# Pooled attention with a soft mixture of experts: a running maximum folded through PSUM, queries pooled in place, shared small buffers, a 24th early weight piece, and a new order of the instructions

## The chip, the cores and the metric

The kernel runs on one core of one Trainium2 chip. The metric is the device time of one execution in microseconds (us). Before the change it is 986.83 us, the median of three runs (986.08 to 987.94). The engines are named as the profile names them: PE is the matrix engine (PEld its weight loads), DVE the vector engine, ACT the scalar engine, POOL the general engine (GpSimd), SP the engine whose queue issues all the DMAs here.

## What is computed

Attention over 64 heads (batch 8, 8 heads, 1152 positions, 64 dimensions), where each two neighbouring queries are first averaged, so that 576 queries per head remain. Its output, 4608 rows of 512, goes through a soft mixture of 8 experts with 4 slots each.

```
q_pool = q.reshape(B, H, S // 2, 2, D).mean(axis=3)
scores = scale * q_pool @ k^T
attn   = softmax(scores, axis=-1)
x      = attn @ v                    # rows: all queries of all batches
logits = x @ phi                     # 32 slots
d      = softmax(logits, axis=0);  slot_input = d.T @ x
slot_out[e] = max(slot_input[e] @ w1[e], 0) @ w2[e]
c      = softmax(logits, axis=1);  out = c @ slot_out
```

All values are 32-bit floats.

## The kernel before

**Tiles.** Two heads form a pair (32 pairs, four of them in a batch). A pair's 576 pooled queries are cut into three units of 192, so there are 96 units, twelve in each of the eight batches. The keys lie in nine chunks of 128. A unit's scores are made in five tiles, of two chunks each and the last of one chunk, with keys on the partitions: a tile `sc` has the form 128 x (2 heads x up to 384) and takes two PSUM banks. There are two such tiles, used in turn.

**A unit, step by step**, with the names of the planner (left) and the tiles that a profile shows:

- `S`: PE makes a score tile (`sc<-qs,k`). A matmul of 32-bit data is recorded as two instructions, so a chunk of two heads is four.
- `C`: ACT copies the tile into SBUF (`s<-sc`).
- `X`: DVE takes the maximum of the tile and the running maximum `M` (`M<-sc,s` for the second tile, where the first is read from its copy in `s`, then `M<-sc,M`). `M` holds two maxima side by side, one for the even and one for the odd chunks. For the last tile, a single chunk, only the even half is touched.
- `Xf`, the fold: DVE takes the maximum of the two halves of `M` (`M<-M`). Before the change it stands between the fourth tile's `X` and the last one's.
- `mt`, `mc`, `mb`: the maximum over keys is finished by three PE transposes (`m<-ident,M`), a DVE reduction (`mc<-m`) and three transposes that spread it (`m<-ident,mc`).
- `sub`, `exp`: DVE subtracts (`s<-s,m`, three groups of three chunks), ACT takes the exponential (`s<-s`).
- `av`: PE multiplies with the values (`U<-s,v`, nine chunks); `add`: POOL adds up eight of the nine chunks (`cs`), and `sums`: PE sums the ninth and POOL's sum over the keys (`m<-s,ones`, `m<-cs,ones`).
- `tc`, `eps`, `rcp`, `tr`, `nx`: the denominator is turned (DVE `zt<-m`), offset (ACT `rc<-zt,eps`), inverted (DVE `rc<-rc`), spread (DVE `rr<-rc`) and multiplied in (POOL `xT<-rr,Us`), and ACT empties the `U` bank (`ue`: `Us<-U`).

**Loads.** For each pair SP issues loads of `k`, `q` and `v`. The raw queries `q` (both of a pair of neighbours, 576 KB) go into one buffer `qt`, and the sum of neighbours (`qs`) is written by POOL (by DVE for the first pair) into one of two buffers that belong to the even and the odd pairs. The two halves of the experts' weights come in 64 pieces of 512 KB. 23 of them have space during the attention and are loaded early; 21 more go into the space that the attention leaves; the last 20 take the place of pieces that have been used.

**The second stage.** When a batch's twelve units are done, the slots' logits, their exponentials and the weighted sums of the rows are made for that batch (`lT`, `eN`, `cN`, `xn`, `slot`), in between the next batch's units. After the last batch follow the experts (`b<-w,sT`, `b<-w,hT`) and the output (`ob`, 24 DMAs).

**What sets the order.** `graph` lists every step with its engine, an assumed cost, what it depends on and a due time made from the table `K["t"]`; `plan` walks through them, engine by engine, and takes among the steps that could start within a small tolerance (`K["wait"]`) the one with the earliest due time, where a matmul of the shape last used is favoured by `K["stay"]`. Each engine then runs its steps in the order that comes out. What an engine really waits for is set by semaphores.

Of the kernel before, what the change touches and what calls it, by code (L numbers as in the profile page):

```python
# [9 lines left out]
F32 = mybir.dt.float32  # L10
F32R = mybir.dt.float32r
AF = mybir.ActivationFunctionType
ALU = mybir.AluOpType
# [9 lines left out]
K = dict(  # L23
    unit=9.0,
    bufs=3,
    stay=97.457,
    wait=dict(PE=0.13, ACT=0.445, DVE=0.179, Pool=4.882),
    adds=(7, 7, 2),
    more=3,
    tiles=((0, 1), (2, 3), (4, 5), (6, 7), (8,)),  # L30
    groups=((0, 1, 2), (3, 4, 5), (6, 7, 8)),
    t=dict(
        S=(1044.713, -27.378, 661.778, 130.467, 574.088),
        C=(225.408, -176.587, 488.066, 26.318, 184.372),
        X=(-718.744, -301.904, -170.628, 686.571, 208.197),
        Xf=(730.727,),
        mt=(148.202,),
        mc=(-195.597,),
        mb=(131.38,),
        sub=(-1080.957, -16.471, 937.631),  # L40
        exp=(-1246.656, 343.957, 478.305),
        add=(-198.042, -184.679, 499.318, 714.631, 189.507, 204.651, 492.919, -541.643, -599.421),
        av=(778.115, -59.256, -118.326, -753.912, 731.892, 755.181, 926.264, 54.633, -257.777),
        sums=(248.993, -468.15, 546.677, -343.84, -281.108, -244.636, -433.554, -1124.137, 780.762, 473.892),
        ue=(756.065,),
        tc=(-949.47,),
        eps=(-191.284,),
        rcp=(26.863,),
        tr=(550.849,),
        ad2=(-53.911, -555.751, -604.838, -526.867, -758.418, 550.551, -1200.835, -328.898, -440.675),  # L50
        nx=(106.946,),
        ldk=(-619.286,),
        ldq=(598.38,),
        ldv=(-572.603,),
        qs=(673.048,),
        lg=(-347.354, 583.603, 769.132, 771.621),
        to=(568.435, 368.579, 194.047, -715.38),
        cb=(-19.617, 862.666),
        rm=(693.434, 659.42),
        nm=(-571.082,),  # L60
        ex=(723.911,),
        ns=(-235.664,),
        ce=(449.167,),
        cz=(641.165,),
        cm=(218.808,),
        on=(-345.56, 611.94, -1045.413, -114.604, -959.343, -369.874, 674.366, 739.505, 216.76, -1205.971, -784.9,
            231.495),
        we=(175.597, 148.186),
        ga=(550.866, 285.942, 446.335),
        end_lg=(297.494, 404.708, 205.171, -617.161),  # L70
        end_to=(-1060.395, 611.733, 617.206, 387.095),
        end_cb=(452.212, 686.767),
        end_rm=(-41.937, 690.132),
        end_nm=(-764.111,),
        end_ex=(794.722,),
        end_ns=(1693.028,),
        end_ce=(-656.049,),
        end_cz=(283.723,),
        end_cm=(-111.35,),
        end_on=(-245.398, -314.311, 700.307, -568.747, 642.619, -769.575, 431.084, 234.287),  # L80
        end_we=(196.041, -1145.853),
        end_ga=(619.182, -375.889, -765.507),
        fin_lg=(193.516, 208.183),
        fin_to=(-933.237, -176.561),
        fin_cb=(677.952, 123.947),
        fin_rm=(47.158,),
        fin_nm=(-321.662,),
        fin_ex=(537.275,),
        fin_ns=(474.34,),
        fin_ce=(684.257,),  # L90
        fin_cz=(538.018,),
        fin_cm=(778.587,),
        fin_on=(655.715, -822.063, -169.447, 107.564),
        fin_we=(557.048, -643.386),
        fin_ga=(827.62, -315.564, 319.142),
        fin_gs=(-237.215,),
    ),
)
LAT = 0.05
# [26 lines left out]
def graph(K, B, HP, NT3, Q, NW):  # L126
# [38 lines left out]
    for n in range(NP):  # L165
        lastu = NT3 * (n - 1) - 1
        k0 = None if n else first
        dma(("ldq", n), 2.0 if n else 0.6, [old(n, "qs", n - 1), ("qs2",) if n == 1 else None], k0)
        dma(("ldk", n), 2.0 if n else 0.8, [old(n > 1, "S", lastu, len(TI) - 1)], k0)
        if n == 0:  # L170
            dma(("k2",), 0.9, [], first)
            dma(("ldv", n), 2.0, [], first)
            dma(("q2",), 1.2, [], first)
            op(("qs2",), "DVE", dve_t((NT3 - 1) * Q), [("x", "q2")], key=0.0)
        else:
            dma(("ldv", n), 2.0, [old(n > 1, "av", lastu, NC - 1)])
        cost = pool_t(NT3 * Q) if n else dve_t(Q)
        op(("qs", n), "Pool" if n else "DVE", cost, [("x", "ldq", n), old(n > 1, "S", lastu, len(TI) - 1)])
    for u in range(NU):
        n, na = u // NT3, adds[u]  # L180
        for i, tl in enumerate(TI):
            g = len(TI) * u + i - 2
            d = [old(g >= 0, "C", g // len(TI), g % len(TI)), old(g >= 0 and g % len(TI), "X", g // len(TI), g % len(TI))]
            d += [("S", u, i - 1)] if i else [("qs", n), ("x", "ldk", n), old(u, "S", u - 1, len(TI) - 1)]
            d += [("x", "k2")] if u == 0 and tl[0] == KF else [("qs2",)] if (u, i) == (1, 0) else []
            op(("S", u, i), "PE", 0.00168 * Q * len(tl), d)
            d = [("S", u, i)]
            for c in tl:
                d += [("av", u - NB, c), freed(u - NB, c)] if u >= NB else []
            op(("C", u, i), "ACT", act_t(2 * Q * len(tl)), d)  # L190
            if i:
                before = ("X", u, i - 1) if 1 < i < len(TI) - 1 else ("C", u, 0) if i == 1 else ("Xf", u)
                op(("X", u, i), "DVE", dve_t(2 * Q * len(tl)), [("C", u, i), before] + [old(u and i == 1, "mt", u - 1)])
            if i == len(TI) - 2:
                op(("Xf", u), "DVE", dve_t(2 * Q), [("X", u, i)])
        b = ("m", u)
        op(("mt", u), "PE", 0.33, [("X", u, len(TI) - 1)], b, take=True)
        op(("mc", u), "DVE", (0.465, 0.55), [("mt", u), old(u > 1, "mb", u - 2)], b)
        op(("mb", u), "PE", 0.34, [("mc", u)], b)
        for g, cs in enumerate(GR):  # L200
# [126 lines left out]
    return order, start, max(free.values())  # L327


NW2 = 21  # L330
NW = 23


class InOrder:
# [15 lines left out]
def pooled_attention_soft_moe(ctx: ExitStack, tc: tile.TileContext, q, k, v, phi, w1, w2, out):  # L350
# [36 lines left out]

    SI4 = const.tile([P, 4, NS], F32, name="SI4")
    idv = ident.rearrange("p (g s) -> p s g", g=4)
    SI = const.tile([P, NS], F32, name="SI")  # L390
    nc.vector.tensor_reduce(SI, idv, axis=AX.X, op=ALU.add)
    for g in range(4):
        nc.vector.tensor_copy(SI4[:, g, :], SI)
    SI4f = SI4.rearrange("p g s -> p (g s)")
    phis = const.tile([P, HP, NS], F32, name="phis")
# [66 lines left out]
    class Pair:  # L462
# [11 lines left out]
            sp_q.dma_start(self.kt[:, KF * P:], k[self.n, :, KF * P:])  # L474

        def load_q(self):
            self.qt = ld.tile([P, 2, SP], F32, name=f"q{self.n}", tag="qt")
            n = SP if self.n else QU
            sp_q.dma_start(self.qt[:, :, :n], q[self.n, :, :, :n])

        def load_q2(self):
            sp_q.dma_start(self.qt[:, :, QU:], q[self.n, :, :, QU:])

        def load_v(self):
            self.vt = vp[self.n % 2].tile([P, 2, NC, D], F32, name=f"v{self.n}", tag="vt")
# [2 lines left out]
                sp_q.dma_start(phis, phi.rearrange("(c p) s -> p c s", p=P))  # L488

        def pool_q(self):  # L490
            self.qs = kp[self.n % 2].tile([P, SP], F32, name=f"qs{self.n}", tag="qs")
            n = SP if self.n else QU
            (pool if self.n else dve).tensor_tensor(self.qs[:, :n], self.qt[:, 0, :n], self.qt[:, 1, :n], op=ALU.add)

        def pool_q2(self):
            dve.tensor_tensor(self.qs[:, QU:], self.qt[:, 0, QU:], self.qt[:, 1, QU:], op=ALU.add)

    xTs = {}

    class Unit:  # L500
# [22 lines left out]
        def maxi(self, i):  # L523
            if i == 1:
                self.M = un.tile([P, 2, 2, QU], F32, name=f"M{self.u}", tag="M", bufs=1)
            n = len(TI[i])
            ps = self.ps[i][:, :, :n * QU].rearrange("p h (c q) -> p c h q", c=n)
            if n == 2:
                dve.tensor_tensor(self.M, ps, self.s[:, 0:2] if i == 1 else self.M, op=ALU.max)
            else:  # L530
                dve.tensor_tensor(self.M[:, 0], ps[:, 0], self.M[:, 0], op=ALU.max)

        def fold(self):
            dve.tensor_tensor(self.M[:, 0], self.M[:, 0], self.M[:, 1], op=ALU.max)

        def max_cols(self, bank):
            M = self.M[:, 0].rearrange("p h q -> p (h q)")
# [78 lines left out]
    class Moe:  # L616
# [11 lines left out]
        def logits(self, hf, phase, bank):  # L628
            cs, n = self.cols(hf)
            pl = mbank[bank]  # L630
            if phase == 0:
                if self.lT is None:
                    if self.last:
                        self.lT = sm.tile([P, self.nt * NQ], F32, name=f"lT{self.i}", tag="lTl", bufs=1)
                    else:
                        self.lT = sm.tile([P, SP], F32, name=f"lT{self.i}", tag="lT", bufs=1)[:, :self.nt * NQ]
                j0 = self.halves[hf][0]
                for hp in range(HP):
                    pe.matmul(pl[NS * hp:NS * hp + NS, :n], phis[:, hp, :], xTs[self.b][:, hp, j0 * NQ:j0 * NQ + n],
                              start=True, stop=True, skip_group_check=True, tile_position=(0, NS * hp))  # L640
            elif phase == 1:
                act.copy(self.lT[:, cs], pl[:, :n])
# [68 lines left out]
        def weights(self, phase, bank):  # L711
            if phase == 0:
                self.turned(bank)
            elif phase == 1:
                if self.last:
                    self.eN = sm.tile([NQ, self.nt, NS], F32, name=f"eN{self.i}", tag="eNl", bufs=1)
                else:
                    self.eN = sm.tile([NQ, NJ, NS], F32, name=f"eN{self.i}", tag="eN", bufs=1)[:, :self.nt]
                act.copy(self.eN, mbank[bank][:NQ, :self.nt * NS].rearrange("p (j s) -> p j s", j=self.nt))
# [244 lines left out]
```

## Time and profile before

One profiled execution took 987.6 us; its span from the first to the last instruction is 985.8 us. The kernel before has a median of 986.83 us.

| engine | busy us | share of the span | instructions |
|---|---|---|---|
| PE | 951.1 | 96% | 9358 |
| PEld | 676.1 | 69% | 9358 |
| DVE | 902.6 | 92% | 1307 |
| ACT | 762.3 | 77% | 1120 |
| POOL | 794.9 | 81% | 815 |

The page's second part shows the span in 40 slices of 24.6 us, each digit being the busy share in tenths:

```profile
PE   6999999999999999999999999999999999999995
...
DVE  5999999999999999999999999999999999999423
ACT  4878888888878888788878788778878788877323
POOL 2899888898889898898889988899888988888200
...
DMA  5132232232223222223122212121221221123898
```

Slices 2 to 37 are the attention with the second stage woven in: PE and DVE are nearly full throughout, DMA is light. In the last three slices, the experts and the output, DMA is full and DVE is not. A row of groups is read as line, engine, operation, out<-in, shapes, count | busy time, mean ns of one | idle time of the engine just before them and what ended it. All rows carry line 344, that of a helper that issues every instruction, so the names of the tiles tell the steps apart.

### The profile page before, as it was taken

How to read it: one execution, taken by the hardware profiler on the slowest of the kernel's cores; microseconds unless marked ns; L12 is line 12 of the kernel's file. 1: busy time of each engine (PE TensorE's matmuls, PEld its weight loads, DVE VectorE, ACT ScalarE, POOL GpSimd, SP SyncE). 2: the span in 40 equal slices, each digit the busy share in tenths (PEclk: the TensorE clock that was granted, in tenths of full speed). 3: DMA queues.
4: the chain of work that ended last, by engine and by line, in shares of the span. 5: the costliest groups of instructions: out<-in, count | busy, mean ns of one | idle time of the engine just before them, and what ended most of it. 6: DMA issues, size and time to landing. Idle time of an engine off the chain costs nothing.

```text
span 985.8 us, 23762 instructions
## 1 busy us (share of the span) xinstructions
PE 951.1 (96%) x9358; PEld 676.1 (69%) x9358; DVE 902.6 (92%) x1307; ACT 762.3 (77%) x1120; POOL 794.9 (81%) x815
## 2 busy tenths in 40 slices
PE   6999999999999999999999999999999999999995
PEld 4666777767776777677777677777776677776542
DVE  5999999999999999999999999999999999999423
ACT  4878888888878888788878788778878788877323
POOL 2899888898889898898889988899888988888200
PEclk8999999999999999999999999999999999999998
DMA  5132232232223222223122212121221221123898
GB/s 171 49 116 82 83 116 82 84 115 74 92 71 116 94 99 88 95 70 117 52 70 73 73 49 68 55 74 52 70 74 54 68 74 49 49 90 128 320 409 339
DMA packets 27681, 101.22 MB, mean 103 GB/s; under 512 B 3505, under 2 KB 4017, under 8 KB 27569
## 3 DMA queue, kind: packets, MB, share of 16 engines
q1 hardware_dynamic: 27568, 99.69, 29.4%
q8 instruction: 74, 1.21, 0.5%
q14 instruction: 39, 0.31, 0.1%
HBM read 90.24 MB, written 9.44 MB: 101 GB/s over the span
## 4 chain that ended last, share of the span: by engine, by line
PE 84%; DVE 12%; issue 1%; ACT 0%; DMA 0%; SPq 0%; DVEq 0%; ACTq 0%
PE sc L344 32%; PE U L344 27%; PE m L344 20%; DVE M L344 7%; PE b L344 5%; DVE s L344 2%; DVE zt L344 1%; DVE mc L344 1%; DVE slot L344 0%; DVE rc L344 0%; ACT s L344 0%; DMA k<-in_k_dram 0%; PE idle L344 0%; DVE c L344 0%; DVE rr L344 0%
## 5 line engine op out<-in xcount | busy, mean ns | idle before, releaser
L344 POOL TENSOR_TENSOR cs<-cs,s 128x384 f32<-128x384 f32 x571 | 586.8, 1028 | 61.7 <-ACT s L344 26.3
L344 ACT COPY s<-sc 128x768 f32<-128x768 f32 (+1 forms) x480 | 344.6, 733 | 91.8 <-PE sc L344 86.1
L344 PE MATMUL sc<-qs,k 64*128 64x192 f32 x3456 | 389.0, 349 | 20.9 <-DVE M L344 16.3
L344 DVE TENSOR_TENSOR s<-s,m 128x1152 f32<-128x1152 f32 x288 | 382.3, 1338 | 3.3 <-PE m L344 2.3
L344 ACT ACTIVATE s<-s 128x1152 f32<-128x1152 f32 x288 | 336.2, 1168 | 45.3 <-DVE s L344 45.1
L344 PEld LDWEIGHTS sc<-qs,k 64*128 64x128 f32 x3456 | 275.6, 188 | 117.0 <-issue 73.8
L344 PE MATMUL U<-s,v 128*64 128x192 f32 x3456 | 344.6, 333 | 0.9 <-ACT Us L344 0.9
L344 PEld LDWEIGHTS U<-s,v 128*64 128x64 f32 x3456 | 227.7, 136 | 73.3 <-issue 47.6
L344 DVE TENSOR_TENSOR M<-sc,M 128x768 f32<-128x768 f32 (+1 forms) x288 | 235.3, 817 | 6.3 <-ACT s L344 2.5
L344 POOL TENSOR_TENSOR cs<-s 128x384 f32<-128x384 f32 x96 | 96.8, 1008 | 33.9 <-ACT s L344 33.8
L344 DVE TENSOR_TENSOR M<-sc,s 128x768 f32<-128x768 f32 x96 | 91.0, 947 | 4.3 <-ACT s L344 4.3
L344 DVE TENSOR_TENSOR M<-M 128x384 f32<-128x384 f32 x96 | 71.2, 742 | 0.3
L344 POOL TENSOR_TENSOR xT<-rr,Us 128x192 f32<-128x192 f32 x95 | 57.1, 601 | 12.7 <-DVE rr L344 10.2
L344 POOL TENSOR_TENSOR qs<-q 128x576 f32<-128x576 f32 x31 | 54.6, 1761 | 13.3 <-DMA q<-in_q_dram 13.3
L344 DVE TENSOR_REDUCE mc<-m 128x3 f32<-128x384 f32 x96 | 53.4, 556 | 11.4 <-PE m L344 7.4
L344 PE MATMUL m<-ident,M 128*128 128x128 f32 x288 | 52.8, 293 | 0.0
L344 PE MATMUL m<-ident,mc 128*128 128x128 f32 x288 | 51.9, 289 | 0.0
L344 PE MATMUL m<-s,ones 128*64 128x192 f32 x388 | 48.7, 330 | 0.2 <-ACT s L344 0.2
L344 PE MATMUL m<-cs,ones 128*64 128x192 f32 x384 | 47.5, 326 | 0.0
L344 ACT COPY Us<-U 128x192 f32<-128x192 f32 x96 | 30.7, 320 | 21.7 <-PE U L344 20.9
L344 PEld LDWEIGHTS m<-ident,mc 128*128 128x128 f32 x288 | 29.2, 136 | 26.6 <-DVE mc L344 24.1
L344 PEld LDWEIGHTS m<-ident,M 128*128 128x128 f32 x288 | 30.1, 141 | 21.6 <-issue 21.6
(92 smaller groups left out, 499.6 us busy)
## 6 DMA issues: line engine op xcount, KB each, us to landing
w<-in_moe_w_dram SPq DMA_DIRECT2D x64, 512.0 KB, 5.4
v<-in_v_dram SPq DMA_DIRECT2D x32, 576.0 KB, 3.8
k<-in_k_dram SPq DMA_DIRECT2D x31, 576.0 KB, 3.8
q<-in_q_dram SPq DMA_DIRECT2D x31, 576.0 KB, 3.8
out_dram<-ob SPq DMA_DIRECT2D x24, 384.0 KB, 6.0
q<-in_q_dram SPq DMA_DIRECT2D x1, 384.0 KB, 6.4
k<-in_k_dram SPq DMA_DIRECT2D x1, 320.0 KB, 4.9
k<-in_k_dram SPq DMA_DIRECT2D x1, 256.0 KB, 2.9
```

Of the source, the lines that this page charges most:

```text
L344: return self.tc.keep_in_program_order(op(*args, **kwargs))
```

## The change

- **The fold.** `X` of the last tile writes its maximum back into the score tile in PSUM (`self.top`) instead of into `M`, and `Xf` now comes after it and takes the maximum of `self.top` and the odd half of `M`. So each of the two instructions has one operand in PSUM and one in SBUF, where before the fold had both in SBUF. The transposes `mt` depend on `Xf`, and so does the reuse of the score tile.
- **The queries.** Each load of `q` becomes two DMAs of half the size: one neighbour goes straight into the buffer `qs`, the other into a smaller `qt`, and the sum is made in place. The load therefore has to wait until the pair that used this `qs` buffer before has made its last scores, as the load of `k` already did.
- **Small buffers.** `SI` becomes the first quarter of `SI4` (three copies instead of four); for the last piece of the second stage `lT` and `eN` share the buffers of `zt` and `Us`.
- **The pieces.** With the space won, 24 pieces of weights are loaded early and 20 go into the space that the attention leaves.
- **The order.** All numbers of `K["t"]`, `stay` and `wait` are new.

```diff
 K = dict(
-    stay=97.457,
-    wait=dict(PE=0.13, ACT=0.445, DVE=0.179, Pool=4.882),
+    stay=344.932,
+    wait=dict(PE=0.084, ACT=0.259, DVE=0.255, Pool=0.318),
...
-        S=(1044.713, -27.378, 661.778, 130.467, 574.088),
+        S=(2388.548, -94.193, 2355.419, 2292.606, -219.496),
...
-        dma(("ldq", n), 2.0 if n else 0.6, [old(n, "qs", n - 1), ("qs2",) if n == 1 else None], k0)
+        dma(("ldq", n), 2.0 if n else 0.6, [old(n, "qs", n - 1), ("qs2",) if n == 1 else None, old(n > 1, "S", lastu, len(TI) - 1)], k0)
...
-        op(("qs", n), "Pool" if n else "DVE", cost, [("x", "ldq", n), old(n > 1, "S", lastu, len(TI) - 1)])
+        op(("qs", n), "Pool" if n else "DVE", cost, [("x", "ldq", n)])
...
+            d += [old(g >= 0 and g % len(TI) == len(TI) - 1, "Xf", g // len(TI))]
...
-                before = ("X", u, i - 1) if 1 < i < len(TI) - 1 else ("C", u, 0) if i == 1 else ("Xf", u)
+                before = ("X", u, i - 1) if i > 1 else ("C", u, 0)
...
-            if i == len(TI) - 2:
-                op(("Xf", u), "DVE", dve_t(2 * Q), [("X", u, i)])
+        op(("Xf", u), "DVE", dve_t(2 * Q), [("X", u, len(TI) - 1)])
...
-        op(("mt", u), "PE", 0.33, [("X", u, len(TI) - 1)], b, take=True)
+        op(("mt", u), "PE", 0.33, [("Xf", u)], b, take=True)
...
-NW2 = 21
-NW = 23
+NW2 = 20
+NW = 24
...
-    SI = const.tile([P, NS], F32, name="SI")
+    SI = SI4[:, 0, :]
...
-            self.qt = ld.tile([P, 2, SP], F32, name=f"q{self.n}", tag="qt")
-            n = SP if self.n else QU
-            sp_q.dma_start(self.qt[:, :, :n], q[self.n, :, :, :n])
+            self.qs = kp[self.n % 2].tile([P, SP], F32, name=f"qs{self.n}", tag="qs")
+            self.qt = ld.tile([P, SP], F32, name=f"q{self.n}", tag="qt")
+            self.q_part(slice(0, SP if self.n else QU))
+
+        def q_part(self, r):
+            sp_q.dma_start(self.qs[:, r], q[self.n, :, 0, r])
+            sp_q.dma_start(self.qt[:, r], q[self.n, :, 1, r])
...
-            (pool if self.n else dve).tensor_tensor(self.qs[:, :n], self.qt[:, 0, :n], self.qt[:, 1, :n], op=ALU.add)
+            (pool if self.n else dve).tensor_tensor(self.qs[:, :n], self.qs[:, :n], self.qt[:, :n], op=ALU.add)
...
-                dve.tensor_tensor(self.M[:, 0], ps[:, 0], self.M[:, 0], op=ALU.max)
+                self.top = ps[:, 0]
+                dve.tensor_tensor(self.top, self.top, self.M[:, 0], op=ALU.max)
 
         def fold(self):
-            dve.tensor_tensor(self.M[:, 0], self.M[:, 0], self.M[:, 1], op=ALU.max)
+            dve.tensor_tensor(self.M[:, 0], self.top, self.M[:, 1], op=ALU.max)
...
-                        self.lT = sm.tile([P, self.nt * NQ], F32, name=f"lT{self.i}", tag="lTl", bufs=1)
+                        self.lT = un.tile([P, self.nt * NQ], F32, name=f"lT{self.i}", tag="zt", bufs=1)
...
-                    self.eN = sm.tile([NQ, self.nt, NS], F32, name=f"eN{self.i}", tag="eNl", bufs=1)
+                    self.eN = un.tile([NQ, 3 * self.nt, NS], F32, name=f"eN{self.i}", tag="Us", bufs=1)[:, :self.nt]
```

What the table of numbers does is seen in the rows of each engine. The first place is DVE in a unit that has no work of the second stage beside it, in the middle of the run, before the change (the number behind a name tells one buffer or unit from another):

```order
L344 TENSOR_TENSOR M_4394<-sc_139,M_4394 128x768
L344 STREAM_TRANSPOSE zt_4439<-m_137 128x192
L344 TENSOR_TENSOR M_4394<-M_4394 128x384
L344 RECIPROCAL rc_4445<-rc_4445 128x6
L344 TENSOR_TENSOR M_4394<-sc_138,M_4394 128x384
L344 STREAM_TRANSPOSE rr_4460<-rc_4445 128x192
L344 TENSOR_TENSOR s_140<-s_140,m_135 128x1152
```

and DVE at the same place of the changed kernel:

```order
L344 TENSOR_TENSOR M_4399<-sc_137,M_4399 128x768
L344 STREAM_TRANSPOSE zt_4444<-m_133 128x192
L344 TENSOR_TENSOR sc_136<-sc_136,M_4399 128x2x192
L344 RECIPROCAL rc_4449<-rc_4449 128x6
L344 TENSOR_TENSOR M_4399<-sc_136,M_4399 128x384
L344 STREAM_TRANSPOSE rr_4464<-rc_4449 128x192
L344 TENSOR_TENSOR s_138<-s_138,m_135 128x1152
```

The neighbours are the same; the last tile's maximum now stands where the fold stood, and the fold where that maximum stood.

The second place is PE in such a unit, from its first matmuls with the values to the next unit's scores, before the change:

```order
L344 MATMUL U_5277<-s_142,v_4746 64x192 x8
L344 MATMUL sc_138<-qs_4934,k_4824 128x192 x4
L344 MATMUL U_5277<-s_142,v_4746 64x192 x2
L344 MATMUL sc_139<-qs_4934,k_4824 128x192 x2
L344 MATMUL U_5277<-s_142,v_4746 64x192 x2
L344 MATMUL m_137<-s_142,ones 64x192 x2
L344 MATMUL m_137<-cs_5215,ones 64x192 x2
L344 MATMUL U_5277<-s_142,v_4746 64x192 x6
L344 MATMUL sc_138<-qs_4934,k_4824 128x192 x4
L344 MATMUL sc_139<-qs_4934,k_4824 128x192 x4
L344 MATMUL m_136<-ident,M_5271 128x128 x3
```

and PE at this place of the changed kernel:

```order
L344 MATMUL U_5463<-s_139,v_5028 64x192 x8
L344 MATMUL sc_136<-qs_5108,k_5093 128x192 x4
L344 MATMUL U_5463<-s_139,v_5028 64x192 x2
L344 MATMUL sc_137<-qs_5108,k_5093 128x192 x2
L344 MATMUL m_135<-s_139,ones 64x192 x2
L344 MATMUL m_135<-cs_5398,ones 64x192 x2
L344 MATMUL U_5463<-s_139,v_5028 64x192 x8
L344 MATMUL sc_136<-qs_5108,k_5093 128x192 x4
L344 MATMUL sc_137<-qs_5108,k_5093 128x192 x4
L344 MATMUL m_135<-ident,M_5458 128x128 x3
```

One chunk of `U` has moved from ahead of the two sums to behind them, so the sums, and with them the read of POOL's `cs`, come one chunk earlier.

The third place is POOL where a pair's queries are summed, before the change:

```order
L344 TENSOR_TENSOR cs_6608<-s_142 128x384
L344 TENSOR_TENSOR cs_6608<-cs_6608,s_142 128x384
L344 TENSOR_TENSOR qs_6627<-q_6390 128x576
L344 TENSOR_TENSOR xT_5985<-rr_6641,Us_6639 128x192
L344 TENSOR_TENSOR cs_6608<-cs_6608,s_142 128x384 x5
```

and POOL there in the changed kernel:

```order
L344 TENSOR_TENSOR cs_6535<-cs_6535,s_139 128x384 x2
L344 TENSOR_TENSOR xT_5993<-rr_6573,Us_6571 128x192
L344 TENSOR_TENSOR cs_6535<-cs_6535,s_139 128x384 x4
L344 TENSOR_TENSOR qs_6549<-qs_6549,q_6550 128x576
L344 TENSOR_TENSOR cs_6633<-s_140 128x384
```

The sum of the queries has moved from among a unit's adds to the place between two units. At the start of the program SP now issues two loads of queries, not one, ahead of the first load of `k`.

More of the change, by code (lines that the diff above doesn't have):

```diff
@@ L32 @@
     t=dict(
-        S=(1044.713, -27.378, 661.778, 130.467, 574.088),
[L34 to L96, printed above, removed]
+        S=(2388.548, -94.193, 2355.419, 2292.606, -219.496),
+        C=(2649.137, 2739.454, 3306.242, 2568.215, 2210.822),
@@ new lines @@
+        X=(-718.744, 41.55, 2544.783, 3038.773, 3019.567),
+        Xf=(2420.829,),
+        mt=(108.212,),
+        mc=(2834.326,),
+        mb=(357.261,),
+        sub=(2554.368, 2777.459, 3141.454),
+        exp=(2989.515, 2742.131, 2760.717),
+        add=(-198.042, 2806.366, 2691.244, 2455.169, 2982.071, 2750.805, 2789.269, 2832.224, -599.421),
+        av=(2746.723, 2428.358, 2392.407, 122.273, 2706.594, 2907.997, 2728.152, 193.704, -87.967),
+        sums=(248.993, -468.15, 101.759, -343.84, -281.108, -244.636, -433.554, 32.153, 2812.114, 369.166),
@@ new lines @@
+        ue=(2111.732,),
+        tc=(2995.475,),
+        eps=(-193.75,),
+        rcp=(-83.517,),
+        tr=(2755.622,),
+        ad2=(-53.911, -555.751, -604.838, -526.867, 2247.684, 2996.492, 85.086, -328.898, -440.675),
+        nx=(2766.587,),
+        ldk=(324.978,),
+        ldq=(3216.414,),
+        ldv=(-24.147,),
+        qs=(2956.952,),
+        lg=(2368.498, 2686.237, 3086.901, 182.464),
+        to=(3083.591, 2792.944, 2930.818, 2510.319),
+        cb=(2719.978, 2928.296),
+        rm=(2748.01, 258.088),
@@ new lines @@
+        nm=(2832.009,),
+        ex=(-128.418,),
+        ns=(2772.413,),
+        ce=(3121.69,),
+        cz=(2769.817,),
+        cm=(3200.587,),
+        on=(3097.6, 2506.278, 3054.228, 446.422, 2486.677, 2547.485, 2860.756, -93.424, 3100.505, 2694.192,
+            3179.786, 243.542),
+        we=(2631.977, 2680.618),
+        ga=(2926.036, 2801.7, 2712.536),
+        end_lg=(3020.693, -97.35, 2441.615, 2619.398),
+        end_to=(2726.63, -63.379, 2652.638, 2157.507),
+        end_cb=(101.937, 2494.248),
@@ new lines @@
+        end_rm=(2678.247, 2864.44),
+        end_nm=(2374.775,),
+        end_ex=(2655.735,),
+        end_ns=(2969.979,),
+        end_ce=(2929.199,),
+        end_cz=(3117.05,),
+        end_cm=(2896.398,),
+        end_on=(2567.266, 2821.336, 2621.07, 2651.936, 2871.573, 3152.89, 2747.133, 2424.348),
+        end_we=(2627.177, 2721.688),
+        end_ga=(2869.597, -375.889, 2849.104),
+        fin_lg=(2808.896, 3072.292),
+        fin_to=(2543.921, 2224.667),
+        fin_cb=(3639.957, 2729.612),
@@ L97 @@
+        fin_rm=(3023.064,),
+        fin_nm=(3006.424,),
+        fin_ex=(2881.713,),
+        fin_ns=(2929.914,),
+        fin_ce=(3322.203,),
+        fin_cz=(3098.918,),
+        fin_cm=(2739.156,),
+        fin_on=(3812.858, 3235.474, 3085.749, 2848.33),
+        fin_we=(3149.484, 2802.356),
+        fin_ga=(2993.364, -315.564, 2524.846),
+        fin_gs=(3664.586,),
     ),
@@ L389, in pooled_attention_soft_moe @@
     idv = ident.rearrange("p (g s) -> p s g", g=4)
-    SI = const.tile([P, NS], F32, name="SI")
+    SI = SI4[:, 0, :]
     nc.vector.tensor_reduce(SI, idv, axis=AX.X, op=ALU.add)
-    for g in range(4):
+    for g in range(1, 4):
         nc.vector.tensor_copy(SI4[:, g, :], SI)
@@ L476, in load_q @@
         def load_q(self):
-            self.qt = ld.tile([P, 2, SP], F32, name=f"q{self.n}", tag="qt")
-            n = SP if self.n else QU
-            sp_q.dma_start(self.qt[:, :, :n], q[self.n, :, :, :n])
+            self.qs = kp[self.n % 2].tile([P, SP], F32, name=f"qs{self.n}", tag="qs")
[4 more added lines that the diff above has]
+            sp_q.dma_start(self.qt[:, r], q[self.n, :, 1, r])
         def load_q2(self):
-            sp_q.dma_start(self.qt[:, :, QU:], q[self.n, :, :, QU:])
+            self.q_part(slice(QU, SP))
         def load_v(self):
@@ L490, in pool_q @@
         def pool_q(self):
-            self.qs = kp[self.n % 2].tile([P, SP], F32, name=f"qs{self.n}", tag="qs")
             n = SP if self.n else QU
-            (pool if self.n else dve).tensor_tensor(self.qs[:, :n], self.qt[:, 0, :n], self.qt[:, 1, :n], op=ALU.add)
+            (pool if self.n else dve).tensor_tensor(self.qs[:, :n], self.qs[:, :n], self.qt[:, :n], op=ALU.add)
         def pool_q2(self):
-            dve.tensor_tensor(self.qs[:, QU:], self.qt[:, 0, QU:], self.qt[:, 1, QU:], op=ALU.add)
+            dve.tensor_tensor(self.qs[:, QU:], self.qs[:, QU:], self.qt[:, QU:], op=ALU.add)
     xTs = {}
```

## The prediction

> **What bounds the kernel.** I first read the shares of the chain of waits, followed back from the end, and two stretches of twelve units each in the middle of the run (columns: stretch, length, busy time of PE, PEld, DVE, ACT, POOL, clock, DMA share, GB/s).
>
> ```profile
> PE 84%; DVE 12%; issue 1%; ACT 0%; DMA 0%; SPq 0%; DVEq 0%; ACTq 0%
> ```
>
> ```profile
> 457.21:570.17 112.96, 111.48 (x1102) 81.01 (x1104) 110.23 (x157) 93.00 (x136) 99.64 (x102) 1.00 0.22 69
> 683.15:796.14 112.99, 111.50 (x1103) 81.01 (x1104) 110.21 (x157) 93.03 (x136) 99.63 (x102) 1.00 0.21 64
> ```
>
> A batch of twelve units takes 113.0 us. PE is busy for 111.5 of them, DVE for 110.2: both are nearly full, and the chain runs on PE with detours over DVE. How much a faster DVE can give is therefore read from PE's idle time. The groups of PE from 35 to 903 us show it (last column):
>
> ```profile
> L344 PE MATMUL sc<-qs,k 64*128 64x192 f32 x3328 | 370.8, 346 | 11.2 <-DVE M L344 11.2
> L344 PE MATMUL U<-s,v 128*64 128x192 f32 x3344 | 333.2, 333 | 0.0
> ```
>
> Scores wait 11.2 us in all for DVE's `M`; the list of waits counts 23 of them. The other groups in that answer show 0.0. One such wait, from the timeline (start, duration, engine):
>
> ```profile
> 753.77 0.38 DVE L344 STREAM_TRANSPOSE zt<-m 128x192 f32<-128x192 f32 x1
> 754.01 2.27 POOL L344 TENSOR_TENSOR cs<-cs,s 128x384 f32<-128x384 f32 x2
> 754.08 1.35 DVE L344 TENSOR_TENSOR M<-M 128x384 f32<-128x384 f32 x1
> ...
> 754.63 0.92 PE L344 MATMUL sc<-qs,k 64*128 64x192 f32 x8
> ...
> 755.46 0.56 DVE L344 TENSOR_TENSOR M<-sc,M 128x384 f32<-128x384 f32 x1
> ...
> 756.17 0.92 PE L344 MATMUL sc<-qs,k 64*128 64x192 f32 x8 [0.62 <-DVE M L344]
> ```
>
> The fold takes 1.35 us beside an add of POOL, the last maximum starts late, and the score tile that it frees is what PE waits for. One unit on, the fold takes 0.52 us and PE runs through:
>
> ```profile
> 763.67 0.52 DVE L344 TENSOR_TENSOR M<-M 128x384 f32<-128x384 f32 x1
> ```
>
> ```profile
> 764.22 1.62 PE L344 MATMUL sc<-qs,k 64*128 64x192 f32 x16
> 765.78 0.55 PE L344 MATMUL m<-ident,M 128*128 128x128 f32 x3
> ```
>
> **The fold.** The rows of `M`, `s` and `cs` (duration min/median/max in ns) show which instructions stretch:
>
> ```profile
> L344 DVE TENSOR_TENSOR M<-sc,s x96: 940/948/958, 8.3 to 897.3; 128x768 f32<-128x768 f32 x96
> L344 DVE TENSOR_TENSOR M<-M x96: 515/552/1360, 12.1 to 902.9; 128x384 f32<-128x384 f32 x96
> ```
>
> ```profile
> L344 DVE TENSOR_TENSOR s<-s,m x288: 1312/1345/1355, 18.3 to 911.1; 128x1152 f32<-128x1152 f32 x144
> ```
>
> ```profile
> L344 POOL TENSOR_TENSOR cs<-cs,s x571: 990/1007/1426, 22.1 to 912.4; 128x384 f32<-128x384 f32 x191
> ```
>
> With one operand in PSUM an instruction of DVE varies by under 45 ns; with both in SBUF, as POOL's adds have them, it reaches 1360. The means by shape:
>
> ```profile
> L344 DVE TENSOR_TENSOR M<-sc,M 128x768 f32<-128x768 f32 x192 | 182.3, 949 | 4.3 <-ACT s L344 2.5
> ...
> L344 DVE TENSOR_TENSOR M<-M 128x384 f32<-128x384 f32 x96 | 71.2, 742 | 0.3
> ...
> L344 DVE TENSOR_TENSOR M<-sc,M 128x384 f32<-128x384 f32 x96 | 53.1, 553 | 2.0 <-PE U L344 0.3
> ```
>
> The new fold has the form of the last of these rows: 742 - 553 = 189 ns less, times 96 = 18.1 us of DVE work. Against it PE can give back only its 11.2 us. Each wait costs a little more than its idle time, because the last matmul's record covers a piece of it: the tile at 754.63 would have been followed after 0.78 us, half of the 1.56 from 764.22 to 765.78 in which two tiles run, so at 755.41; the next came at 756.17, 0.76 late for 0.62 shown. Of this surplus I take half, a factor of 1.1: the term is -12.3 us if all these waits go. Better end: -11.2 x 0.76 / 0.62 = -13.7.
>
> Whether a further wait is late next: in that place the fold must lose the 0.76; 1.35 - 0.55 = 0.80. It just does.
>
> [...]
>
> The write of the last maximum into PSUM stands in no row. If it costs as the read does, 553 stays. If a bank must be read and written in turn, the 384 elements cost like 768: 949, plus 396. I take 553, the same size and shape, and keep 949 as a rival.
>
> The last maximum now waits for ACT's copy earlier in DVE's row. In the quiet units the copy is long done; beside the second stage it is not:
>
> ```profile
> 695.87 1.00 DVE L344 TENSOR_TENSOR M<-M 128x384 f32<-128x384 f32 x1
> 695.89 0.48 ACT L344 COPY s<-sc 128x384 f32<-128x384 f32 x1 [0.26 <-PE sc L344]
> ...
> 696.97 0.56 DVE L344 TENSOR_TENSOR M<-sc,M 128x384 f32<-128x384 f32 x1
> ```
>
> There the first of the two could start at 695.89 + 0.48 = 696.37, and two of 0.55 end at 697.47; before it was 697.53. So DVE idles but nothing comes later: 0, with an upper end of 0.5 us in 3 of 12 units, 24 x 0.5 = +12.
>
> **The sums and POOL.** Ahead of a unit's two sums PE now has one chunk of `U` less, so POOL's `cs` must be ready that much sooner. The chain prices it, with the change of shape:
>
> ```profile
> 752.07 0.53 PE sc L344 x4
> 752.60 0.47 PE U L344 x4
> 753.07 0.67 PE m L344 x8
> ```
>
> POOL has time in most units, but not where it also sums queries (31 times): there its adds follow each other without a gap until they are needed:
>
> ```profile
> 745.32 1.78 POOL L344 TENSOR_TENSOR qs<-q 128x576 f32<-128x576 f32 x1
> 747.07 0.60 POOL L344 TENSOR_TENSOR xT<-rr,Us 128x192 f32<-128x192 f32 x1
> 747.62 5.36 POOL L344 TENSOR_TENSOR cs<-cs,s 128x384 f32<-128x384 f32 x5
> ```
>
> They end at 752.98, and PE's `m` starts at 753.07 in the chain: no time to spare. Between two units POOL idles 0.35 us,
>
> ```profile
> 770.38 1.00 POOL L344 TENSOR_TENSOR cs<-s 128x384 f32<-128x384 f32 x1 [0.35 <-ACT s L344]
> ```
>
> which `qs`, now put there, can use. So 0.47 - 0.35 = 0.12 us is short, x 31 = +3.7; ends 0 and 0.47 x 31 = +14.6. Behind POOL's adds wait the sum on PE and all of PE behind it.
>
> **Loads.** SP issues 32 more in the middle, where DMA is 0.2 busy: nothing. A load now waits for scores and lands some us later; POOL's sum stands after a whole unit of adds, over 7 us on. If it is late, it stands in the term above. At the start the second load of queries pushes the first `k` back by one issue of about 0.6 us, and PE's first matmul waits for just that `k`:
>
> ```profile
> 0.74 0.66 SPq L344 DMA_DIRECT2D q<-in_q_dram  x1
> 1.46 1.05 SPq L344 DMA_DIRECT2D k<-in_k_dram  x2
> ```
>
> ```profile
> 4.47 4.01 PE L344 MATMUL sc<-qs,k 64*128 64x192 f32 x24 [4.47 <-DMA k<-in_k_dram]
> ```
>
> That is +0.6 (0 to +1). A copy of `SI` less runs ahead of the first load's arrival: 0.
>
> **Changes of shape on PE.** The chain's pieces price them:
>
> ```profile
> 796.14 2.10 PE U L344 x24
> ...
> 800.54 1.50 PE sc L344 x16
> ```
>
> Twenty more `U` instructions cost 2.10 - 0.47 = 1.63, 0.326 a chunk, so entering `U` costs 0.15; for scores (1.50 - 0.53) / 3 = 0.323, entering 0.21. Over the whole order the entries into scores go from 343 to 360, into `U` or sums from 242 to 219, into full-array matmuls, the transposes above all, from 205 to 211, with 5125 matmuls in both: 17 x 0.21 - 23 x 0.15 + 6 x 0.15 = +1.0.
>
> **The 24th piece and the shared buffers.** In the last part PE computes without a break, so it does not wait for weights, and the DMAs are full from 935 on (same columns as above):
>
> ```profile
> 930.00:935.00 5.00, 5.00 (x52) 1.48 (x48) 0.00 (x0) 0.54 (x1) 0.00 (x0) 1.00 0.70 220
> 935.00:965.00 30.00, 29.99 (x374) 13.91 (x370) 7.26 (x28) 7.78 (x19) 0.00 (x0) 1.00 1.02 406
> ```
>
> Both kernels have 44 places, so both move the last 20 pieces and the output after PE has used the first. What comes early leaves a gap at 930 to 935, where DMA is 0.70 busy already: 0. If it counted, 0.524 MB at 406 GB/s = -1.3. `lT` and `eN` of the last piece need buffers whose last use lies before theirs on the same chain: 0.
>
> **Sum.** -12.3 + 3.7 + 0.6 + 1.0 = -7.0, from the profiled 987.6 to 980.6; that execution lies 0.8 over the median of 986.83, so the median is forecast at 979.8. With the better ends (-13.7, 0, 0, and -1.3 for the piece, beside the 1.0) it would be 972.8.
>
> **Rivals.**
> 1. *Nothing much:* contention goes, but the waits come back at POOL's `cs` (+14.6) or at ACT's copy (+12). With two thirds of POOL's end the sum is -12.3 + 9.7 + 0.6 + 1.0 = -1.0, so 985.8. For: POOL has no time to spare in a third of the units. Against: it idles in the others and catches up.
> 2. *Slower:* the last maximum in PSUM takes 949. Then DVE has 0.396 - 0.189 = 0.207 us a unit more, 20 us in all, where it has 2.8 us of 113 free a batch and its two instructions stand right ahead of PE's wait; at the same idle share the run ends near 1006. It decides from 553 + 189 = 742 on. For: no row shows such a write. Against: reading PSUM costs nothing extra per element, (949 - 553) / 384 = 1.03 ns, where `s<-s,m` over its longer run has 1345 / 1152 = 1.17 with its fixed part.
> 3. *DVE is the bound:* all 18.1 us come off, 968.7. For: DVE's 110.2 and its place ahead of PE's waits. Against: PE's 111.5 stays and its shapes do not change. [...]
> 4. *It does not do what it says:* the new form is stretched by POOL too; time as before plus 5.3, about 992. The spread of the `s<-s,m` row speaks against.
>
> **Chances.** Forecast (974 to 983) 0.55; rival 1 0.20, half of it within 0.2% of before; rival 2 0.07; rival 3 or all waits gone (968 to 974) 0.14; rival 4 and other delays 0.04. A measurement here can tell 0.2%, about 2 us, from no change. Faster 0.79, same 0.10, slower 0.11. For 8 in 10 the range takes the forecast, most of rival 1 and the better half of rival 3: 970 to 987.
>
> **What would show it.** Right: the fold at 553 with a maximum under 600; PE's idle before `sc` from 35 to 903 us near 0; 111 us a batch; the first matmul 0.6 later; the stretch from the experts' first matmul (928.17 before) to the end unchanged. Wrong: the write at over 600; idle before `m<-cs`; entries that cost more than counted. The forecast falls if PE's waits merely change their name.

## The result, and the profile after

The changed kernel takes 965.46 us, the median of four runs (963.49 to 966.90), beside 986.46 us for the kernel before (four runs, 985.89 to 987.94). The ratio is 0.9779 with a 95% interval of 0.9761 to 0.9797: 21.0 us less, where 7.0 were forecast. The profiled execution is the one of 963.49 us, its span 961.7.

The shares of the chain of waits of the changed kernel, and two stretches of twelve units each (length, busy time of PE, PEld, DVE, ACT, POOL, granted clock, DMA share, GB/s):

```profile
PE 96%; DVE 1%; issue 1%; ACT 0%; DMA 0%; SPq 0%; DVEq 0%
```

```profile
471.07:581.55 110.48, 110.48 (x1101) 81.27 (x1100) 107.25 (x157) 92.71 (x137) 96.69 (x102) 1.00 0.20 67
692.03:802.51 110.48, 110.48 (x1101) 81.32 (x1100) 107.24 (x157) 92.78 (x137) 96.65 (x102) 1.00 0.20 66
```

The detours over DVE have left the chain (12% before, 1% now). A batch takes 110.5 us instead of 113.0, PE is never idle in it, and DVE has 3.2 us free. The groups of PE in the stretch from 35 to 903 us:

```profile
L344 PE MATMUL sc<-qs,k 64*128 64x192 f32 x3324 | 367.2, 345 | 0.0
L344 PE MATMUL U<-s,v 128*64 128x192 f32 x3404 | 330.1, 331 | 0.0
```

The 11.2 us of idle time before the scores are gone and no other group has taken them over. The rows of DVE and POOL behind that, in the list of groups by shape:

```profile
L344 DVE TENSOR_TENSOR sc<-sc,M 128x384 f32<-128x384 f32 x96 | 51.6, 537 | 1.3 <-ACT s L344 0.2
...
L344 DVE TENSOR_TENSOR M<-sc,M 128x384 f32<-128x384 f32 x96 | 52.3, 545 | 0.1
```

```profile
L344 POOL TENSOR_TENSOR cs<-cs,s 128x384 f32<-128x384 f32 x571 | 574.0, 1005 | 50.7 <-ACT s L344 15.6 <-POOL cs L344 2.0
...
L344 POOL TENSOR_TENSOR qs<-qs,q 128x576 f32<-128x576 f32 x31 | 43.9, 1418 | 12.8 <-DMA q<-in_q_dram 12.3 <-PE m L344 0.4
```

The fold costs 545 ns (742 before), the last maximum, now written into PSUM, 537. POOL has become faster too: its sum of the queries takes 1418 ns, where the one quoted in the prediction took 1.78 us.

**Where the 21 us came from.** Units 12 to 83 (from the reduction `mc` of unit 11 to that of unit 83, a place that both kernels have) are six batches. The stretch before, with its row of scores, and the stretch after:

```profile
115.71:793.47 677.76, 669.25 (x6602) 486.06 (x6601) 660.80 (x930) 558.07 (x810) 598.28 (x607) 1.00 0.24 79
```

```profile
L344 PE MATMUL sc<-qs,k 64*128 64x192 f32 x2592 | 287.9, 346 | 8.5 <-DVE M L344 8.5
```

```profile
111.09:773.36 662.27, 662.27 (x6597) 487.41 (x6600) 642.34 (x930) 555.66 (x810) 580.55 (x607) 1.00 0.24 82
```

677.76 - 662.27 = 15.49 us for 72 units, and x 96/72 = 20.7 for all 96. The two profiled spans differ by 24.1 us (985.8 - 961.7); what the steady rate leaves of that lies at the start and at the end; the start alone moves by some us (the changed kernel reaches the `mc` of unit 11 at 111.09 us, the same kernel with 23 pieces of weights at 112.86). So nearly the whole gain is made at a steady rate in the attention. Yet the row of scores shows only 8.5 us of idle time to win there. This gap is what the experiments had to explain. The starts of PE's instructions place it: in these stretches the times from one score matmul's start to the next one's add up to 213.2 us before and 197.8 after, 15.4 less; all else together differs by 0.1. The split is rough, because the new order has 15 fewer such pairs (2319 for 2334); an experiment below sets matmul against matmul.

### The profile page after: what moved, and what is told of

Same layout as the page of the kernel before. It is cut to its first block, busy times and chain, and to the rows that moved or that the text cites. A ratio compares the mean times of both kernels' runs of the same rounds, so it can differ in the third digit from the quotient of the medians.

```text
span 961.7 us, 23870 instructions
## 1 busy us (share of the span) xinstructions
PE 940.4 (98%) x9358; PEld 675.9 (70%) x9358; DVE 879.2 (91%) x1306; ACT 758.7 (79%) x1120; POOL 771.0 (80%) x815
## 4 chain that ended last, share of the span: by engine, by line
PE 96%; DVE 1%; issue 1%; ACT 0%; DMA 0%; SPq 0%; DVEq 0%
PE sc L344 37%; PE U L344 32%; PE m L344 23%; PE b L344 5%; DVE M L344 1%; DMA k<-in_k_dram 0%; PE idle L344 0%; ACT s L344 0%; ACT lT L344 0%; DVE mc L344 0%; SPq L344 0%; ACT xkt L344 0%; DVE sc L344 0%; DVE ob L344 0%; ACT xqs L344 0%
## 5 line engine op out<-in xcount | busy, mean ns | idle before, releaser
L344 POOL TENSOR_TENSOR cs<-cs,s 128x384 f32<-128x384 f32 x571 | 574.0, 1005 | 50.7 <-ACT s L344 15.6
L344 PE MATMUL sc<-qs,k 64*128 64x192 f32 x3456 | 383.9, 347 | 9.6 <-DMA k<-in_k_dram 4.9
L344 PE MATMUL U<-s,v 128*64 128x192 f32 x3456 | 335.8, 331 | 0.2 <-ACT s L344 0.2
L344 PEld LDWEIGHTS U<-s,v 128*64 128x64 f32 x3456 | 231.9, 136 | 64.8 <-issue 38.0
L344 POOL TENSOR_TENSOR qs<-qs,q 128x576 f32<-128x576 f32 x31 | 43.9, 1418 | 12.8 <-DMA q<-in_q_dram 12.3
L344 DVE TENSOR_TENSOR sc<-sc,M 128x384 f32<-128x384 f32 x96 | 51.6, 537 | 1.3 <-ACT s L344 0.2
```

What stands on the lines that cost most here:

```text
L344: return self.tc.keep_in_program_order(op(*args, **kwargs))
```

## The experiments

Theory 1: the fold with two operands in SBUF, beside POOL's adds, cost the 21 us, and the profile's idle column shows only part of what PE loses to it. Theory 2: the new order did it. Theory 3: the queries summed in place made POOL faster, and that did it. Each ratio below is to runs of the kernel before on the same chip, with its 95% interval.

**The operand in SBUF again, all else as changed.**

```diff
-                self.top = ps[:, 0]
-                dve.tensor_tensor(self.top, self.top, self.M[:, 0], op=ALU.max)
+                dve.tensor_tensor(self.M[:, 0], ps[:, 0], self.M[:, 0], op=ALU.max)
...
-            dve.tensor_tensor(self.M[:, 0], self.top, self.M[:, 1], op=ALU.max)
+            dve.tensor_tensor(self.M[:, 0], self.M[:, 0], self.M[:, 1], op=ALU.max)
```

> The changed kernel, with its order of instructions and its queries and pieces, but the unit's last maximum is written to M in SBUF again, so that the fold reads two operands in SBUF. Theory 1 (the fold beside GpSimd in SBUF cost the 21 us, because the idle time that the page shows before TensorE's waits is less than what they cost): the fold's mean goes from 545 ns to 700 or more with single ones over 1000, TensorE gets its waits before the scores back, and the time is 980 to 986. Theory 2 (the new order did it, the place of the operand is nothing): folds may be long again, but TensorE does not wait, and the time is 965 to 968. Theory 3 (the queries summed in place, GpSimd shorter): 965 to 968 as well.

Measured: 978.29 us, ratio 0.9915 (0.9900 to 0.9929). Some 13 of the 21 us come back, more than theory 2 allows and a little less than theory 1 wanted. The stretch of units 12 to 83, its rows of PE, and DVE's fold, of this kernel:

```profile
115.16:785.90 670.74, 663.89 (x6593) 486.81 (x6592) 656.35 (x931) 557.03 (x809) 593.59 (x607) 1.00 0.24 81
```

```profile
L344 PE MATMUL sc<-qs,k 64*128 64x192 f32 x2588 | 285.2, 345 | 0.3
...
L344 PE MATMUL m<-ident,mc 128*128 128x128 f32 x216 | 38.7, 288 | 6.5 <-DVE mc L344 6.4
```

```profile
L344 DVE TENSOR_TENSOR M<-M 128x384 f32<-128x384 f32 x96 | 82.1, 855 | 0.1
```

The fold is long again (855 ns in the mean), but PE does not wait before the scores: it waits before the transposes that spread the maximum, since the fold now stands right ahead of `mt`. So the place of the fold decides where its length is paid. At the steady rate of these 72 units the kernel loses 670.74 - 662.27 = 8.5 us to the changed one and keeps 677.76 - 670.74 = 7.0 of the gain. Two folds of this kernel, DVE and POOL from the timeline, show how it gets long:

```profile
438.77 1.30 DVE L344 TENSOR_TENSOR M<-M 128x384 f32<-128x384 f32 x1
```

```profile
437.57 2.09 POOL L344 TENSOR_TENSOR cs<-cs,s 128x384 f32<-128x384 f32 x2
```

```profile
457.61 0.56 DVE L344 TENSOR_TENSOR M<-M 128x384 f32<-128x384 f32 x1
```

```profile
456.59 2.43 POOL L344 TENSOR_TENSOR cs<-cs,s 128x384 f32<-128x384 f32 x2
```

The first fold starts 0.11 us after an add of POOL (the second of the two, at 438.67) and takes 1.30. The second starts 0.08 before an add (at 457.69); it takes 0.56, and that add takes 1.34 instead of 1.00. The one that comes second waits until the other is nearly done. Over the folds of this kernel that began 0.1 to 0.66 us into an add, length plus offset is constant: 1311 + 101, 1193 + 218, 954 + 460, 754 + 664 ns, and all others between 1410 and 1424. A fold ends some 415 ns after the add that it met, so it was free to go on some 0.10 to 0.15 us before that add's end (alone it takes 515 to 560 ns); folds that began 0.88 us or more into an add were not held up (at most 560 ns).

**The new code with the old table, and the old code with the new table.**

```diff
-    stay=344.932,
-    wait=dict(PE=0.084, ACT=0.259, DVE=0.255, Pool=0.318),
+    stay=97.457,
+    wait=dict(PE=0.13, ACT=0.445, DVE=0.179, Pool=4.882),
...
-        S=(2388.548, -94.193, 2355.419, 2292.606, -219.496),
+        S=(1044.713, -27.378, 661.778, 130.467, 574.088),
...
```

> The changed kernel with the table of numbers of before (due times, stay, wait), so that the code and the planner's rules are new and the order is what they give with the old table. Theory 1: 965 to 970, since the fold has its operand in PSUM. Theory 2: 980 to 988. Theory 3: 965 to 970.

Measured: 1196.32 us, ratio 1.2122 (1.2080 to 1.2163). The reverse, the kernel before with the new table (the same lines with + and - exchanged):

> The kernel of before with the new table of numbers, its code and its planner's rules as they were. Theory 1: 983 to 990, the fold still takes 742 ns in the mean and TensorE still waits before the scores. Theory 2: 965 to 970. Theory 3: 983 to 990.

Measured: 1046.63 us, ratio 1.0607 (1.0591 to 1.0622).

**The maximum alone,** with its rules, in the kernel before and with the old table:

```diff
+            d += [old(g >= 0 and g % len(TI) == len(TI) - 1, "Xf", g // len(TI))]
...
-            if i == len(TI) - 2:
-                op(("Xf", u), "DVE", dve_t(2 * Q), [("X", u, i)])
+        op(("Xf", u), "DVE", dve_t(2 * Q), [("X", u, len(TI) - 1)])
...
-                dve.tensor_tensor(self.M[:, 0], ps[:, 0], self.M[:, 0], op=ALU.max)
+                self.top = ps[:, 0]
+                dve.tensor_tensor(self.top, self.top, self.M[:, 0], op=ALU.max)
...
-            dve.tensor_tensor(self.M[:, 0], self.M[:, 0], self.M[:, 1], op=ALU.max)
+            dve.tensor_tensor(self.M[:, 0], self.top, self.M[:, 1], op=ALU.max)
```

> The kernel of before with the maximum alone changed: the fold after the last tile, one operand in PSUM, the order's rules as this needs, the old table, queries as before, 23 pieces. Theory 1: 966 to 972. Theory 2: 983 to 990. Theory 3: 983 to 990, since GpSimd's sums of the queries still take 1.78 us and its column sums end late in every third unit.

Measured: 1194.34 us, ratio 1.2146 (1.2078 to 1.2214). No theory had expected these three. The timeline of this last kernel tells why (DVE, then PE):

```profile
408.23 0.92 DVE L344 TENSOR_TENSOR M<-sc,M 128x768 f32<-128x768 f32 x1
409.08 1.33 DVE L344 TENSOR_TENSOR s<-s,m 128x1152 f32<-128x1152 f32 x1
410.34 0.17 DVE L344 RECIPROCAL rc<-rc 128x6 f32<-128x6 f32 x1
410.43 0.53 DVE L344 TENSOR_TENSOR sc<-sc,M 128x384 f32<-128x384 f32 x1
410.88 0.36 DVE L344 STREAM_TRANSPOSE rr<-rc 128x192 f32<-128x192 f32 x1
411.17 0.52 DVE L344 TENSOR_TENSOR M<-sc,M 128x384 f32<-128x384 f32 x1
```

```profile
411.83 1.65 PE L344 MATMUL sc<-qs,k 64*128 64x192 f32 x8 [1.70 <-DVE M L344]
```

The fold is short here, but the old table, under the new rules, puts a whole subtraction (1.33 us) between the fourth tile's maximum and the last one's, and PE waits 1.70 us for the score tile that the fold frees. PE's granted clock is lower too, 0.949 in the mean beside 0.992 before (the tile at 411.83 takes 1.65 us, where one in the changed kernel at a granted clock of 1.00 takes 0.92): an estimated 1191 x 0.043 = 51 us of the 207 lost. In the changed kernel no subtraction stands there, and the scores run through:

```profile
402.54 0.95 DVE L344 TENSOR_TENSOR M<-sc,M 128x768 f32<-128x768 f32 x1
403.53 0.38 DVE L344 STREAM_TRANSPOSE zt<-m 128x192 f32<-128x192 f32 x1
403.84 0.54 DVE L344 TENSOR_TENSOR sc<-sc,M 128x384 f32<-128x384 f32 x1
```

The table and the rules belong together; a table that was made for other rules costs 60 to 210 us. So these three say that the order matters much, but not how the 21 us divide, and a cleaner test of theory 1 had to keep the old order to the letter.

**The old order, one operand of the fold in PSUM.** The fourth tile's maximum is made in two halves, one of them written into the scores' own bank, and the fold in its old place reads that:

```diff
-            if n == 2:
+            if i == len(TI) - 2:
+                self.top = ps[:, 0]
+                dve.tensor_tensor(self.M[:, 1], ps[:, 1], self.M[:, 1], op=ALU.max)
+                dve.tensor_tensor(self.top, self.top, self.M[:, 0], op=ALU.max)
+            elif n == 2:
...
-            dve.tensor_tensor(self.M[:, 0], self.M[:, 0], self.M[:, 1], op=ALU.max)
+            dve.tensor_tensor(self.M[:, 0], self.top, self.M[:, 1], op=ALU.max)
```

> The kernel of before, its order and table to the letter, but the fold in its old place reads one operand in PSUM: the maximum of the fourth tile is made in two halves of 384 elements, M in SBUF for one and the scores' own bank for the other (some 140 ns longer together, one more instruction of VectorE for each unit), and the fold takes the one from PSUM and the other from M. Theory 1: all folds take 515 to 560 ns, the queries' sum 1.42 us, TensorE's waits before the scores go, and the time is 966 to 972 with the old order. Theory 2 (the new order did some 8 us of the 21, the operand 13): 972 to 978. Rival (the bank of the fourth tile is held until the fold has ended, and TensorE now waits for that): 980 to 990.

Measured: 982.86 us, ratio 0.9948 (0.9935 to 0.9962), inside the range of the rival. But its parts are those of theory 1. The stretch of units 12 to 83 and its row of scores:

```profile
121.36:790.98 669.62, 665.25 (x6602) 487.26 (x6601) 650.81 (x1003) 555.91 (x810) 580.75 (x607) 1.00 0.24 80
```

```profile
L344 PE MATMUL sc<-qs,k 64*128 64x192 f32 x2592 | 280.5, 343 | 4.4 <-DVE M L344 1.5 <-ACT rc L344 0.9 <-DVE rc L344 0.3
```

PE's instructions are the same as before, in the same order, so each start can be set beside its own of before. From score matmul to score matmul they need 197.3 us in place of 213.2: 15.9 less, as much as the changed kernel wins there. So the waits before the scores go with the operand alone. But 7.7 us come back at one other place, from `U` to the next unit's first scores, so that 8.1 are left (677.76 - 669.62). The timeline of that place (DVE, then PE):

```profile
399.84 0.57 DVE L344 TENSOR_TENSOR sc<-sc,M 128x384 f32<-128x384 f32 x1
400.31 0.37 DVE L344 STREAM_TRANSPOSE zt<-m 128x192 f32<-128x192 f32 x1
400.61 0.52 DVE L344 TENSOR_TENSOR M<-sc,M 128x384 f32<-128x384 f32 x1
```

```profile
399.90 1.15 PE L344 MATMUL U<-s,v 128*64 128x192 f32 x12
401.23 1.57 PE L344 MATMUL sc<-qs,k 64*128 64x192 f32 x16 [0.18 <-ACT rc L344]
```

The next unit's first score tile uses the bank of the fourth tile, which the fold now holds until 401.13; the scores start 0.10 later. The profile names `rc`, which also ended about then and which the scores do not read; at all 48 places in these units where PE loses time there, the fold had ended 55 to 146 ns before the scores. So the rival's mechanism is real, at half the price of what is won. The rest of this kernel's time lies at the start, where PE waits twice over 1 us and the granted clock falls then (PE's rows, and the stretch from 36 to 44 us with the clock ahead of the DMA share):

```profile
35.40 0.92 PE L344 MATMUL sc<-qs,k 64*128 64x192 f32 x8 [1.05 <-ACT rc L344]
37.64 1.65 PE L344 MATMUL sc<-qs,k 64*128 64x192 f32 x8 [1.31 <-DVE M L344]
```

```profile
36.00:44.00 8.00, 6.68 (x38) 4.50 (x37) 5.59 (x9) 3.68 (x5) 4.88 (x6) 0.57 0.15 59
```

The second tile takes 1.65 us for the first one's 0.92. By estimate the clock costs 8 x 0.43 = 3.4 us there; before, it was 1.00 from 36 to 44 us. Unit 4 is reached 6.9 us later than before, and the rest of these 6.9 was not traced. One of the six runs took 978.98 us; why is not known.

**The queries alone, in place, in the kernel before.**

```diff
-            sp_q.dma_start(self.qt[:, :, :n], q[self.n, :, :, :n])
+            sp_q.dma_start(self.qs[:, r], q[self.n, :, 0, r])
+            sp_q.dma_start(self.qt[:, r], q[self.n, :, 1, r])
...
-            (pool if self.n else dve).tensor_tensor(self.qs[:, :n], self.qt[:, 0, :n], self.qt[:, 1, :n], op=ALU.add)
+            (pool if self.n else dve).tensor_tensor(self.qs[:, :n], self.qs[:, :n], self.qt[:, :n], op=ALU.add)
```

> The kernel of before with its order and its maximum, but the queries by two transfers, one of them straight into the tile where they are summed in place. Theory 1: the sum stays at 1.7 to 1.8 us, because the fold in SBUF still runs beside it, and the time is 985 to 989. Theory 3: the sum falls to 1.42 us and the time to 978 to 983.

Measured: 987.95 us, ratio 1.0004 (0.9995 to 1.0012). And **the queries out of place in the changed kernel** (the same lines the other way round, with 23 pieces to make room):

> The changed kernel with its order, its maximum in PSUM, but queries loaded by one transfer into a double tile and summed out of place as before, and 23 early weight pieces (which give the room). Theory 1 (the fold's two operands in SBUF cost the 21 us, its own length and the POOL sums beside it alike): the queries' sum takes 1.40 to 1.45 us without any change in place, and the time is that of e6 within 1 us, 965 to 968. Theory 3 (summing in place makes GpSimd faster): the sum is back at 1.78 us, GpSimd's column sums are late in every third unit, and the time is 4 to 8 us above e6.

Measured: 963.59 us, ratio 0.9761 (0.9747 to 0.9775). POOL's sum of the queries, in place in the first kernel and out of place in the second:

```profile
L344 POOL TENSOR_TENSOR qs<-qs,q 128x576 f32<-128x576 f32 x31 | 54.5, 1759 | 12.6 <-DMA q<-in_q_dram 12.6
```

```profile
L344 POOL TENSOR_TENSOR qs<-q 128x576 f32<-128x576 f32 x31 | 44.0, 1418 | 13.4 <-DMA q<-in_q_dram 13.1 <-PE m L344 0.2
```

In place or not does nothing: theory 3 falls. What takes 0.35 us from the sum is the fold with two operands in SBUF, which ran beside 30 of the 31 sums before; with the old order and queries and one operand of the fold in PSUM, the sum takes 1.41 us.

**23 pieces in the changed kernel.**

```diff
-NW2 = 20
-NW = 24
+NW2 = 21
+NW = 23
```

> The changed kernel with 23 early weight pieces in place of 24, nothing else. If the 24th piece counts as the weights' stream at the end suggests (one piece of 0.5 MB at some 380 GB/s is 1.3 us): 966.5 to 967.5. If it counts nothing, as the forecast took it: 965 to 966.

Measured: 964.88 us, ratio 0.9772 (0.9759 to 0.9784), beside 0.9779 with 24: the piece is worth nothing that can be told, and the queries' form (0.9761) hardly more.

## Why the prediction was wrong, step by step

- **The fold's waits: -12.3 forecast, some -21 measured** (15.9 x 96/72 = 21.2 by the matched matmuls; the whole steady rate is 20.7). The mechanism was right: contention with POOL makes the fold long (up to 1360 ns for 515 to 560 alone), the last maximum late, and PE waits for its tile; with an operand in PSUM these waits go, and with the new order none comes in their place. The size was wrong, and the step that failed is "Against it PE can give back only its 11.2 us": the idle column was read as the price of the waits, but for a small surplus. Two parts of it:
  - *The surplus on each wait.* The prediction took a factor of 1.1. But every wait costs about the same amount more than it shows, since a score tile's record lasts 0.92 us where PE, running on, starts the next tile 0.75 us after it. Set beside the same matmuls in the kernel with the old order and the operand in PSUM, the 19 waits in units 12 to 83 show 8.5 us and cost 12.2, each some 0.2 us more than it shows, whether that is 0.25 or 0.63. The score matmuls right behind them, which start anew, lose another 1.5. The tile at 756.17 came 0.79 us late for 0.62 shown, and 0.89 was lost by the end of its pair.
  - *Time that shows as 0.0.* The other 15.9 - 13.7 = 2.2 us in these units lie in delays of 20 to some 100 ns of score matmuls that show no wait. The column does not see them, and the prediction took 0.0 as no wait. What PE waits for there was not traced.
- **POOL: +3.7 forecast, nothing measured.** The step took 1.78 us as the length of the sum of the queries. It was 1.42 with a fold in its way. The change took that away too, so POOL got earlier where the prediction had it short by 0.12; PE's idle time before `m<-cs` is 0.0. The term counted one end of the contention (the fold) and kept the other (POOL's share) as a fixed cost.
- **The first `k`: +0.6 forecast.** PE's first matmul comes at 4.95 us, 4.47 before, +0.48. That is not clear of the spread between executions: it comes at 4.61 in the kernel before with two loads of queries, and at 4.72 in the kernel with the old order and the operand in PSUM, which has one. Later it is lost among other differences of the start (the granted clock from 10 to 20 us was 0.66 before and 1.00 after), so its worth at the end was not measured.
- **Changes of shape: +1.0 forecast, some +0.5 measured.** Without its 7.7 us behind `U`, the kernel with the old order and the operand in PSUM would need 669.62 - 7.7 = 661.9 us for units 12 to 83; the changed kernel, which shows no wait, needs 662.27. That is 0.4 more, 0.5 for all units, an estimate.
- **The 24th piece and the end: 0 forecast.** Right for the piece. The experts and the output, from 904.94 on, take 56.8 us in place of 57.6: 0.9 less.
- **The write into PSUM at 553:** 537, right; rival 2 falls. Nor did an operand in PSUM make the fold longer: folds that no add held up take 515 to 560 ns with both operands in SBUF, and 515 to 559 with one in PSUM.
- **Rival 3 (DVE is the bound, 968.7)** comes near in its number, but not by its mechanism: now PE has no idle time and DVE has 3.2 us a batch; DVE's 23.4 us less of busy time (902.6 to 879.2) are not what came off. No rival and no chance was set below 968.
- **The operand and the order.** The prediction gave the whole gain to the operand and only costs to the order. Units 12 to 83 take 677.76 us before, 670.74 with the new order and the fold in SBUF, 669.62 with the old order and the operand in PSUM, and 662.27 with both. x 96/72, the operand is worth 10.8 us in the old order and 11.3 in the new one, the order 9.4 or 9.8: about half each. So theory 1 holds for half of the gain. What the order does is to move the fold away from ahead of the last maximum, and to the one tile whose bank may be held longer. Its other moves (the chunk of `U`, the sum of the queries) were not tried one by one, so their part of the 9 to 10 us stays open.

## What to carry to other kernels

Read a wait on a busy engine by the starts of its instructions against the same instructions running freely, not by the idle column: where records overhang the pace (here 0.92 for 0.75 us), a wait costs more than it shows (12.2 us for 8.5, and 1.5 behind it), and delays of 20 to some 100 ns show nothing. When an instruction stretches because of a neighbour on another engine, look at that neighbour's own rows too, as its stretched length is no fixed cost either (here 1.78 us beside a fold, 1.42 without). And when an operand is moved to memory that something else waits for, move the step to the place where that memory can be held (in its old place the fold gave 7.7 us back), and make the order anew.

## What was not expected of the hardware

- DVE's fold and POOL's adds excluded each other but for about the last 0.1 us of an add: a fold of 515 to 560 ns became up to 1360, or an add of 1000 became 1426, whichever came second (before the change; a fold that began up to 46 ns after POOL's instruction still took 516 or 517); with one operand in PSUM, in the changed kernel, neither moved (515 to 559 and 992 to 1024 ns).
- A maximum that reads and writes the same place in PSUM, with its second operand in SBUF, took 527 to 567 ns for 384 elements (537 in the mean), no more in the mean than one that writes to SBUF (517 to 559, 553 in the mean before the change).
- After two waits of PE of 1.05 and 1.31 us within 3 us, one kernel's granted clock was 0.57 for 8 us. The changed kernel waits 0.94 and 1.15 us at 9.76 and 12.57 and 1.21 at 18.97, and its clock stays at 1.00 from 10 to 26 us. What decides was not tried.
